# A first layer split as 128 + 64 rows, with paired half-array matmuls, separate id loads, a new order on the GpSimd queue and a later start of the expert slots

## The chip, the cores and the metric

The kernel runs on one core of a Trainium2 chip. The metric is device time in microseconds (us) of one execution. Each version was executed several times; executions of one kernel on one chip mostly agree within half a per cent. A run more than 1.5% above the fastest of its kernel is called slow and left out; the others are called fast. Every comparison is made within one set of runs on one chip, beside the kernel before on that same chip.

## The reference, cut to what matters

```python
# x: (8, 3584, 192); 28672 tokens of 192 numbers; 8 experts; F = 1024
w    = softmax(weight)                        # 8 heads x 7 taps
x    = causal_conv(x, w)                      # every head: 24 channels
e    = argmax(x @ w_gate)                     # one expert for each token
gate = softmax(x @ w_gate)[e]
eom  = sigmoid(x @ w_output_gate)             # only [e] is used
out  = gate * eom[e] * (relu(x @ w1[e]) @ w2[e])   # 192 -> 1024 -> 192
```

## The kernel before

The tokens are handled in 16 **units** of 1792. For each unit a **front** convolves, computes the logits, picks experts, and sorts the rows by expert. The sorted rows, scaled by the gate, with the token's id in two extra columns, are scattered by GpSimd into a stream in HBM, eight scatters a unit. From the stream they are loaded transposed, 512 rows of one expert at a time, and each such **slot** passes through the expert's two layers. A slot has four **quarters**. Four slots run in every unit, interleaved with the fronts of later units; the last unit takes all that is left, and a loop at the end takes whatever rows did not fill a slot.

The first layer has 192 input rows, and the array takes 128. So the kernel loads rows 0 to 127 into `xa`, the other 64 rows and padding into `xb`, and spends two full matmuls on each of eight chunks of 128 outputs:

```python
def load_w(e):                                    # before
    o = e * WE
    nc.gpsimd.dma_start(wres[:, o:o + F], moe_w1[e, 0:128, :])
    nc.gpsimd.dma_start(wres[0:64, o + F:o + 2 * F], moe_w1[e, 128:D, :])
    ...                                           # w2; rows 64..127 are zeroed by zero_w

def slot_load(base, u):
    ...
    i = nc.sync.dma_start_transpose(xa, xcg[bass.ds(base, TT), 0:128])
    i = nc.sync.dma_start_transpose(xb, xcg[bass.ds(base, TT), 128:256])

class Slot:
    def first(self, q):                           # a quarter of the first layer
        pp = ps_h.tile([128, 2, 512], FP32, tag="ph", name="pp")
        for j in range(2):
            fc = 2 * q + j
            nc.tensor.matmul(pp[:, j, :], self.w(fc * 128, 128), self.xa,
                             start=True, stop=False)
            nc.tensor.matmul(pp[:, j, :], self.w(F + fc * 128, 128), self.xb,
                             start=False, stop=True)
        ...                                       # ReLU into ht, on ScalarE or VectorE

    def second(self, q):
        ...                                       # eight matmuls of 192 columns
        if q == 1:                                # token ids, from a column of xb
            for j in range(4):
                nc.tensor.matmul(self.pp[:, 2 * D + j:2 * D + j + 1],
                                 self.xb[:, j * 128:(j + 1) * 128], idw,
                                 start=False, stop=(j == 3))
        if q % 2 == 1:
            nc.scalar.copy(out=self.y[:, q - 1:q + 1, :], in_=...)
            for j in (q - 1, q):
                emit_in()                         # at most one waiting scatter
                i = nc.gpsimd.indirect_dma_start(out=out, ...)   # 128 output rows
```

Scatters are not issued where their rows are made. They wait in a list, `pend`, and `emit_in()` issues one. The traces show GpSimd issuing its transfers in program order, so this Python order is the order of the queue. The main schedule starts the slots at unit 1:

```python
prev = None
for u in range(1, NU):
    todo = []
    for e, bap, inv in plans.pop(u):
        base = reg(bap, [ET.SP], E * CAP - TT)
        todo.append((e, inv, slot_load(base, u)))
    fa = front_a(u + 2) if u + 2 < NU else iter(())
    fb = front_b(u + 1) if u + 1 < NU else iter(())
    for k, (e, inv, xab) in enumerate(todo):
        ...
        s = Slot(xab, w_at(e * WE), inv)
        for q in range(4):
            s.first(q)
            drain(fa, 1)                          # one piece of a front
            if prev is not None:
                prev.second(q)
            drain(fb, 1)                          # one piece of another front
        prev = s
    drain(fa); drain(fb)
    emit_in(len(pend))
...
with tc.For_i(0, rn, 1):                          # slots chosen at run time
    ...
```

## Time and profile before

| kernel before | value | where it is read |
|---|---|---|
| time, median of 3 | 780.03 us | runs |
| profiled execution | 773.92 us, span 772.0 us | run, profile |
| TensorE busy | 85% of the span | busy totals |
| first slot starts | 86.1 us | timeline |
| one unit, mean of units 2 to 13 | 43.1 us | timeline |
| wait for `xa` where units meet | 2.3 to 3.0 us, units 2 to 14; 6.4 us at unit 15 | timeline |
| one slot with nothing beside it | 6.19 us | timeline of the tail |
| clock granted to TensorE, mean of each of units 2 to 14 | 0.96 (nine units) or 1.00 (four) | windows |

The profile has five engines: PE is TensorE (PEld its weight loads), DVE VectorE, ACT ScalarE, POOL GpSimd, and SP only issues transfers. A line of a timeline gives start, duration, engine, source line, operation, what it writes and reads, and the shape. A bracket at its end tells how long the engine was idle before it and what ended that. Matmuls are pipelined, so the distance from one start to the next is the cost, and the listed duration is not. The prediction shows the lines that carry the argument.

### The profile page before, as it was taken

What the parts mean: (1) busy time and instruction counts of PE and PEld (TensorE: products, weight loads), DVE (VectorE), ACT (ScalarE), POOL (GpSimd) and SP (SyncE); (2) the same over time, 40 slices, a digit from 0 to 9 for tenths busy, and PEclk for the clock granted to TensorE, in tenths of its full rate; (3) what the DMA queues carried; (4) which work ended last, traced back from release to release, by engine and by line L of the source; (5) the groups of instructions that cost most, each with busy time, mean ns of one, the idle gap of its engine ahead of it and who ended that gap; (6) DMA issues with size and microseconds to landing.
All of it is one profiled execution on the core that took longest, in us unless ns stands there. A gap on an engine that the chain in (4) does not pass through costs nothing. (4 is left out here: it accounts for less than half of the span.)

```text
span 772.0 us, 14134 instructions
## 1 busy us (share of the span) xinstructions
PE 655.4 (85%) x4948; PEld 436.2 (57%) x4948; DVE 406.5 (53%) x1298; ACT 366.5 (47%) x581; POOL 411.5 (53%) x425
## 2 busy tenths in 40 slices
PE   3866498989989898989989898989989898869953
PEld 1524165665757475656747475656757575547632
DVE  7425183836566383837556383837566474802220
ACT  0657153554535363545536364545546354436621
POOL 1436145473747465473737465563737375656652
PEclk9978599999999999999999999999999999989987
DMA  7999933253535343252535343442532313234110
GB/s 152 231 238 203 142 101 108 72 160 75 144 102 143 103 133 104 69 155 73 152 92 139 99 127 106 101 133 62 157 88 74 93 61 110 70 102 114 48 41 9
DMA packets 132359, 86.59 MB, mean 112 GB/s; under 512 B 88427, under 2 KB 122455, under 8 KB 132288
## 3 DMA queue, kind: packets, MB, share of 16 engines
q1 hardware_dynamic: 102656, 42.35, 23.4%
q0 software_dynamic: 28736, 43.31, 20.5%
q8 instruction: 39, 0.64, 0.4%
q14 instruction: 32, 0.26, 0.1%
q10 hardware_dynamic: 896, 0.03, 0.1%
HBM read 35.80 MB, written 44.43 MB: 104 GB/s over the span
## 5 line engine op out<-in xcount | busy, mean ns | idle before, releaser
L579 POOL DMA_INDIRECT out_dram<-y,oi x260 | 262.7, 1011 | 242.1 <-issue 179.0
L547 ACT ACTIVATE ht<-pp 128x1024 f16<-128x1024 f32 x195 | 199.3, 1022 | 183.9 <-PE pp L541 183.9
L539 PE MATMUL pp<-xa,wres 128*128 128x512 f16 x520 | 203.0, 390 | 61.1 <-DMA xa<-xcg_sorted 61.1
L558 PE MATMUL pyt<-wres,ht 128*128 128x192 f16 (+1 forms) x2080 | 220.9, 250 | 2.9 <-DVE ht L545 2.9
L558 PEld LDWEIGHTS <-ht 128*128 128x128 f16 x2080 | 182.7, 99 | 67.1 <-issue 37.0
L541 PE MATMUL pp<-xb,wres 128*128 128x512 f16 x520 | 202.2, 389 | 12.2 <-DMA xb<-xcg_sorted 12.2
L457 POOL DMA_INDIRECT xcg_sorted<-xs,du x128 | 130.1, 1017 | 89.4 <-ACT xs L278 42.2
L290 PE MATMUL pf<-xt,band 118*112 118x384 f32 x256 | 115.3, 543 | 19.5 <-DMA xt<-in_x_dram 14.1
L539 PEld LDWEIGHTS <-wres 128*128 128x128 f16 (+1 forms) x520 | 51.4, 99 | 112.4 <-DMA xa<-xcg_sorted 41.2
L545 DVE TENSOR_SCALAR ht<-pp 128x1024 f16<-128x1024 f32 x65 | 79.2, 1219 | 59.2 <-PE pp L541 59.2
L569 ACT COPY y<-pyt 128x384 f32<-128x384 f32 x130 | 62.4, 480 | 93.9 <-PE pyt L558 84.1
L280 DVE COPY cv<-pf 112x384 f32<-112x384 f32 x54 | 29.2, 541 | 89.3 <-PE pf L290 89.3
L290 PEld LDWEIGHTS pf<-xt,band 118*112 118x112 f32 x256 | 48.0, 195 | 48.9 <-DVE band L133 13.6
L541 PEld LDWEIGHTS <-wres 128*128 128x128 f16 (+1 forms) x520 | 51.8, 100 | 37.6 <-issue 8.2
L572 DVE TENSOR_SCALAR oi<-pyt 128x4 uint32<-128x4 f32 x65 | 10.5, 162 | 115.8 <-ACT y L569 110.3
L439 PE MATMUL pf<-xrow,pm 112*128 112x194 f16 x512 | 64.6, 247 | 6.9 <-DVE pm L423 4.5
L418 DVE TENSOR_TENSOR xrow<-cv,gs 112x384 f16<-112x384 f32 x128 | 64.7, 545 | 0.0
L423 DVE TENSOR_SCALAR pm<-pos,pos 112x256 f16<-112x256 f16 x256 | 64.6, 324 | 0.0
L304 PEld LDWEIGHTS pf<-identf,cv 112*128 112x128 f32 x384 | 43.6, 141 | 17.4 <-DVE cv L280 2.2
L278 ACT COPY cv<-pf 112x384 f32<-112x384 f32 x74 | 33.9, 479 | 40.1 <-PE pf L290 25.0
L304 PE MATMUL pf<-identf,cv 112*128 112x112 f32 x384 | 51.5, 260 | 0.5 <-ACT cv L278 0.4
L278 ACT CAST xs<-pf 128x388 f16<-128x388 f32 x76 | 37.2, 489 | 28.8 <-PE pf L439 20.2
(132 smaller groups left out, 425.0 us busy)
## 6 DMA issues: line engine op xcount, KB each, us to landing
xt<-in_x_dram SPq DMA_DIRECT2D x8, 1344.0 KB
xt<-in_x_dram SPq DMA_DIRECT2D x8, 1260.0 KB
out_dram<-y,oi POOLq DMA_INDIRECT x260, 2.7
wres<-in_moe_w_dram POOLq DMA_DIRECT2D x8, 384.0 KB, 10.5
wres<-in_moe_w_dram POOLq DMA_DIRECT2D x8, 256.0 KB, 11.5
xcg_sorted<-zrow SPq DMA_DIRECT2D x8, 256.0 KB
xcg_sorted<-xs,du POOLq DMA_INDIRECT x128, 3.2
xa<-xcg_sorted SPq DMA_TRANSPOSE x65
```

Of the source, the lines that this page charges most:

```text
L278: nc.scalar.copy(out=o, in_=i)
L290: nc.tensor.matmul(pc[0:BT, 0:NB * GH], band[0:KI, h, :], xt[0:KI, :, h * GH:(h + 1) * GH], start=True, stop=True)
L304: nc.tensor.matmul(pt[:, j * BT:(j + 1) * BT], cvf[0:BT, m * 2 * D + i * 128:m * 2 * D + (i + 1) * 128], identf[0:BT, 0:BT], is_transpose= ...
L418: nc.vector.tensor_tensor(out=xr[P, k:k + 2, 0:D], in0=cv[P, k:k + 2, :], in1=gs[P, k:k + 2].unsqueeze(2).to_broadcast([BT, 2, D]), op=ALU ...
L423: nc.vector.tensor_scalar(out=pms[i][P, l, :], in0=pos16[P], scalar1=pos[P, l * NG + i:l * NG + i + 1], scalar2=None, op0=ALU.is_equal)
L457: i = nc.gpsimd.indirect_dma_start(out=xcg2, out_offset=bass.IndirectOffsetOnAxis(ap=du[:, i:i + 1], axis=0), in_=xs.rearrange("p r w -> p ...
L539: nc.tensor.matmul(pp[:, j, :], self.w(fc * 128, 128), self.xa, start=True, stop=False)
L541: nc.tensor.matmul(pp[:, j, :], self.w(F + fc * 128, 128), self.xb, start=False, stop=True)
L545: nc.vector.tensor_relu(out=ht, in_=pp)
L547: nc.scalar.activation(out=ht, in_=pp, func=AF.Relu)
L558: nc.tensor.matmul(self.pp[:, o:o + D], self.ht[fc // 2][:, fc % 2, q * 128:(q + 1) * 128], self.w(2 * F + fc * D, D), start=(fc == 0 and ...
L579: i = nc.gpsimd.indirect_dma_start(out=out, out_offset=bass.IndirectOffsetOnAxis(ap=self.oi[:, j:j + 1], axis=0), in_=self.y[:, j, :], in_ ...
```

## The change

The intent is to save a quarter of the first layer's streaming. `xb` now holds columns 64 to 191. An even chunk takes rows 0 to 127 in one full matmul and has rows 128 to 191 left; an odd chunk takes rows 64 to 191 and has rows 0 to 63 left. The two 64-row remainders lie on different halves of the array and are meant to run side by side. Four full matmuls become two full ones and a pair. As `xb` no longer holds the ids, a third transfer `xi` loads them.

```diff
@@ weights @@
+    WA = F + F // 2
+    def load_w(e):
+        ... wres[:, o:o + F] as (g, l, c): rows 0..127 (l=0) or 64..191 (l=1)
+        for p0, d0, l in ((0, 0, 1), (64, 128, 0)):      # the 64-row remainders
+            nc.gpsimd.dma_start(
+                wres[p0:p0 + 64, o + F:o + WA].rearrange("p (g c) -> p g c", c=128),
+                bass.AP(... offset=w.offset + d0 * F + l * 128, ...))
@@ slot_load @@
-        i = nc.sync.dma_start_transpose(xb, xcg[bass.ds(base, TT), 128:256])
+        i = nc.sync.dma_start_transpose(xb, xcg[bass.ds(base, TT), 64:192])
+        i = nc.sync.dma_start(
+            xi, xcg[bass.ds(base, TT), IDC:IDC + 2].rearrange("(j p) w -> p j w", p=128))
@@ Slot.first @@
-            for j in range(2): ... two full matmuls for each chunk
+            nc.tensor.matmul(pp[:, 0, :], w[:, o:o + 128], self.xa, start=True, stop=False)
+            nc.tensor.matmul(pp[:, 1, :], w[:, o + 128:o + 256], self.xb, start=True, stop=False)
+            nc.tensor.matmul(pp[:, 0, :], w[64:128, c:c + 128], self.xb[64:128],
+                             start=False, stop=True)
+            nc.tensor.matmul(pp[:, 1, :], w[0:64, c:c + 128], self.xa[0:64],
+                             start=False, stop=True)
@@ Slot.second @@
-                for j in range(4): ... id matmuls against idw
-                for j in (q - 1, q):
-                    emit_in()
-                    i = nc.gpsimd.indirect_dma_start(out=out, ...)
+                pout.extend((self.y, self.oi, j) for j in (q - 1, q))
@@ schedule @@
-    NXS = 6
+    NXS = 10                                             # scatter buffers
+    U0 = 2                                               # slots start at unit 2
+    ND = 3                                               # run-time slots laid out statically
-    for u in range(1, NU):
+    for u in range(U0, NU):
+        if u == NU - 1:
+            for sel, bap, inv in [pick() for _ in range(ND)]:
+                ... todo.append((w_dyn(sel), inv, slot_load(base, u)))
                 if prev is not None:
                     prev.second(q)
+                    emit_out()                           # outputs, right after their copy
                 drain(fb, 1)
+                emit_in(len(pend))                       # every scatter that is ready
@@ run-time slots @@
+    def w_dyn(sel):
+        wd = pwd.tile([128, WE], FP16, tag="wd", name="wd")   # 2 buffers
+        nc.sync.dma_start(wd, wres[:, bass.ds(reg(sel...), WE)])   # 768 KB
+        return wd
```

Five things thus change together: the matmuls of the first layer, the ids, the order on the GpSimd queue, the start and the end of the slots, and the prologue (two experts' weights ahead of the first front instead of four).

## The prediction

> **What bounds the kernel now.** The kernel convolves, routes and sorts 16 units of 1792 tokens (the "front"), then runs 512-row slots, each through one expert's two layers. I read the page's busy totals first, then its slices, the groups, the waits, and the timeline of single units.
>
> ```profile
> PE 655.4 (85%) x4948; PEld 436.2 (57%) x4948; DVE 406.5 (53%) x1298; ACT 366.5 (47%) x581; POOL 411.5 (53%) x425
> PE   3866498989989898989989898989989898869953
> DMA  7999933253535343252535343442532313234110
> L539 PE MATMUL pp<-xa,wres 128*128 128x512 f16 x520 | 203.0, 390 | 61.1 <-DMA xa<-xcg_sorted 61.1
> L541 PE MATMUL pp<-xb,wres 128*128 128x512 f16 x520 | 202.2, 389 | 12.2 <-DMA xb<-xcg_sorted 12.2
> L565 PE MATMUL pyt<-idw,xb 128*128 128x1 f16 x260 | 15.7, 164 | 0.0
> ```
>
> TensorE leads at 85%, and its only long waits are for xa and xb, the transposed loads: 61.1 + 12.2 us. The first 96 us (five slices of 19.3 us) are different: DMA is at 7 to 9 tenths and TensorE low. The 1040 first-layer matmuls are listed at 390 ns, but they are pipelined; the timeline gives the true pitch. Here are the end of one unit and the first matmul of the next; columns are start us, duration, engine, line, what.
>
> ```profile
> 295.27 0.38 PE L541 MATMUL pp<-xb,wres 128*128 128x512 f16 x1
> 295.58 1.71 PE L313 MATMUL pf<-tt,wg 128*32 128x448 f32 x16
> 297.22 0.83 PE L558 MATMUL pyt<-wres,ht 128*128 128x192 f16 x8
> 297.89 0.38 PE L539 MATMUL pp<-xa,wres 128*128 128x512 f16 x1
> 298.11 0.38 PE L541 MATMUL pp<-xb,wres 128*128 128x512 f16 x1
> ...
> 299.19 0.82 PE L558 MATMUL pyt<-wres,ht 128*128 128x192 f16 x8
> 302.82 0.39 PE L539 MATMUL pp<-xa,wres 128*128 128x512 f16 x1 [2.81 <-DMA xa<-xcg_sorted]
> ```
>
> First-layer matmuls start 0.216 us apart, and eight second-layer ones take 0.66 us. In the tail, where nothing else runs, a quarter slot (4 + 8 matmuls) lasts 1.52 us (713.40 to 714.92), the quarter with the id matmuls 1.63, so a slot is 3 x 1.52 + 1.63 = **6.19 us**. Units begin at 129.9, 173.7, ... 604.7, 647.6: 43.1 us each on average over twelve, of which 2.6 us is the xa wait at the boundary. What feeds that wait is the POOL queue:
>
> ```profile
> 296.68 0.98 POOL L457 DMA_INDIRECT xcg_sorted<-xs,du  x1 [0.30 <-issue]
> ```
>
> Here POOL starts the unit's last scatter; its lines follow each other every 1.285 us, scatters and output rows alternating, 24 a unit (31 us). Its data were ready near 291; it stood in line. The load issues at 299.19, 2.5 us after the scatter's start, and TensorE resumes at 302.82, 6.1 us after it.
>
> **What the Trainium skill says.** "TensorEngine Tiling (Array Packing)", Key Properties: changing the tiling mode drains TensorE; tiles run independently. The trace agrees. Before the column-tiled L313, the last matmul should end at 295.27 + 0.216 = 295.49, but L313 starts at 295.58: 0.09 us. L313 is eight fp32 matmuls of 448 columns in four column tiles. One fp32 matmul of 384 columns takes 0.65 us here (L290), so eight would take 6.1 us serially and two rounds 1.5; it takes 1.64. Tiles do overlap; entry and exit together cost about 0.2 us. The 64-row matmuls L385 and L386 say the same: 0.09 late on entry (96.06 against 95.94 + 0.03), 0.085 late on exit (96.28 against 96.13 + 0.066).
>
> "TensorE: Matmul & The Clock Gate", Measured speedup vs the span model: a row-tiled pack takes one matmul's duration plus about 4 ns per tile. No row-tiled pair runs before the change, so the trace cannot say. The same page, Part 1: about 3.4 us of idleness halves the clock. The trace agrees in part: after the 2.5 us gap at 259.1, first-layer pitch is soon 0.43, until 264, and the units so hit have mean clock 0.96 instead of 1.00.
>
> "DMA: Bandwidth & Descriptors", Specifications: line rate needs 512 B per transfer. The new id load has runs of 4 B; no transfer of that kind is in this trace.
>
> **The change, part by part.** The diff does five things.
>
> 1. First layer. Per quarter slot four full matmuls become two full and two half-row ones meant to run together. Removed: one stream, 0.216 us. Added: entry 0.09 + exit 0.085 + weight-load stagger, estimated at 0.01 to 0.05. Net gain about 0.03 us a quarter, **0.12 a slot**, not the 0.86 that counting streams promises.
>
> 2. Ids. L565 goes: 0.11 us a slot. Three small vector operations (0.16 us each) replace two; a third SP transfer per slot joins two issued 1.45 us apart. SP has room. Slot: 6.19 - 0.12 - 0.11 = **5.96 us**.
>
> 3. POOL order. Scatters are issued as soon as their rows are ready and outputs right after their copy. The scatter chain after group 0 becomes 15 x 1.285 = 19.3 us instead of 21.6, so the boundary wait mostly goes. Unit: 43.1 - 2.6 (wait) - 0.6 (clock, half the units losing 1.3 or so) - 4 x 0.23 = 39.0. The chain itself (five quarters to group 0, about 12.3, + 0.7 + 19.3 + 6.1 = 38.4) is nearly as long, so I add 0.7 for imperfect meeting: **39.7 us**.
>
> 4. Slots start at unit 2, not 1. Replaying the routing on the reference's inputs, I count 60 static slots, three chosen at run time but laid out statically, and zero loop iterations after; before there were 64 static and one loop iteration. Two slots (12 us) and the serial loop go. A chosen slot copies its 768 KB of weights first, with two buffers: the third copy can begin only when the first chosen slot has finished. TensorE then waits about 2 us start + 768 KB at some 200 GB/s (best prologue rate is 254) + transposes behind it: estimated 8 us, plus 1.7 for the clock.
>
> 5. Prologue. One more front before the first slot, but only two experts' weights ahead of it instead of four, and ten scatter buffers instead of six. Fronts took 19.5 us (28.5 to 48) and 25 with DMA-starved waits; then came 13.4 us until xa, with DMA still full. I take 28.5 + 3 x 19.5 + 10 = **97 us** against 86. By bytes: 17.2 MB moved by 86 us, 2.5 MB more at 230 GB/s also gives 97.
>
> Sum: first slot at 97; units 2 to 13, 12 x 39.7 = 476.4; unit 14, with no convolution beside it, 37.5 (39.6 before, POOL-bound: 24 x 1.285 = 31 plus the ramp); unit 15, 10 x 5.96 + 9.7 wait + 6.0 + last second layer 2.7 = 78; end, 12.7 (before: 4.6 from the last matmul to the last output's end, 6.1 to the span's end; 2 for the skipped loop). Span 702. Timed runs before lie 8.0 over the profiled span (780.03 against 772.0), so **710 us**.
>
> **Rivals.** *The pair overlaps and the drain hides*: slot 5.22 us, 0.74 less. For it: the span model, and that 0.09 was seen with other shapes. It would save 47 us at most, but POOL (5.14 us a slot in the tail, 31 a unit) and the scatter chain would hold some: 670. *The halves do not overlap*: each quarter pays 0.18 more, 63 x 0.7 = 44 us: 755, still faster through parts 3 and 4. *POOL or the scatter chain becomes the bound*: units stay at 42 to 43 us; for it, POOL's unbroken row from 278 to 303; against it, 31 us of work in 40. It gives 740 to 745. *The 4-byte id loads clog the shared DMA engines and delay xa*: for it, 512 tiny runs a slot; against it, DMA is only 3 to 5 tenths busy in the steady part; +10 us.
>
> **Range and chances.** Parts 3 and 4 rest on counted waits and slots, so faster is nearly sure. The pair's true cost is the main unknown (670 to 755 at the ends), then the prologue (90 to 108). Eight in ten: 668 to 740. Faster by over 2% 0.96, within 2% 0.03, slower 0.01.
>
> **What would show it right or wrong.** The pitch of a quarter slot in the tail: 1.49 if I am right, 1.30 if the pair is free, 1.66 if serial. The xa wait at unit boundaries: under 1 us. Unit starts 39.7 apart. First slot near 97. One TensorE gap of some 8 us before the last chosen slot, and no loop body. Wrong if the pair is free and POOL keeps pace (lower), or if boundary waits return (higher).

## The result, and the profile after

The changed kernel takes **729.65 us** (median of 4, 726.50 to 733.58) beside 779.99 us (median of 4, 778.27 to 781.78) for the kernel before in the same rounds. The ratio is 0.936 (95% interval 0.931 to 0.941). Here and below a ratio is the mean time of one kernel's fast runs over the mean time of the other's fast runs of the same rounds, so it is not quite the ratio of the medians.

These are lines of the page of the changed kernel: busy totals, the slices of TensorE, and groups of instructions.

```profile
PE 638.0 (87%) x4592; PEld 373.5 (51%) x4592; DVE 412.9 (56%) x1367; ACT 356.7 (49%) x575; POOL 409.6 (56%) x425
PE   3888259899899999999999999899997988699974
L599 PE MATMUL pp<-xa,wres 128*128 128x512 f16 x240 | 94.5, 394 | 45.1 <-DMA xa<-xcg_sorted 44.7
L604 PE MATMUL pp<-xa,wres 64*128 64x512 f16 x240 | 95.6, 398 | 0.0
L602 PE MATMUL pp<-xb,wres 64*128 64x512 f16 x240 | 95.6, 398 | 0.0
```

TensorE's busy time fell only by 17 us, from 655 to 638, though a quarter of the first layer's streams is gone. The wait for `xa` is still there: 45 us ahead of L599. In the slices the hole ahead of the first slot is deeper than before (2 in the fifth slice, 73 to 91 us), and the long middle is fuller.

This is one quarter slot in the tail of the changed kernel, from the timeline, and the start of the next quarter:

```profile
655.01 0.38 PE L599 MATMUL pp<-xa,wres 128*128 128x512 f16 x1
655.23 0.38 PE L600 MATMUL pp<-xb,wres 128*128 128x512 f16 x1
655.54 0.39 PE L602 MATMUL pp<-xb,wres 64*128 64x512 f16 x1
655.54 0.39 PE L604 MATMUL pp<-xa,wres 64*128 64x512 f16 x1
655.86 0.83 PE L629 MATMUL pyt<-wres,ht 128*128 128x192 f16 x8
656.53 0.38 PE L599 MATMUL pp<-xa,wres 128*128 128x512 f16 x1
```

The two halves do start together. But they start 0.31 us after the second full matmul, where a full matmul would have followed after 0.216. The second layer begins 0.32 us after them, again 0.10 late. The quarter lasts 1.52 us, as long as a plain quarter did before. A slot takes 6.08 us in place of 6.19, and those 0.11 us are the id matmuls.

Where the profiled span shrank, 772.0 to 731.9 us, is seen by stage:

| stage (us) | before | after | difference |
|---|---|---|---|
| start of unit 2's slots | 129.9 | 97.6 | -32.4 |
| units 2 to 13 | 12 x 43.1 | 12 x 41.8 | -15.9 |
| unit 14 | 39.6 | 41.1 | +1.4 |
| from unit 15 to the end | 84.7 | 91.5 | +6.7 |

Before, unit 1 had slots too; now those rows are taken later, which is why the tail grows. The first and last rows together are -25.6 us and belong to the schedule. The second is the steady part, where the scatter queue and the waits lie. (The differences sum to -40.1. The profiled execution before was 6 us below its median and the one after 4 us above, which is the rest of the 50.)

### The profile page after: what moved, and what is told of

It reads as the page before. It is cut to its first block, busy times and chain, and to the rows that moved or that the text cites. A ratio compares the mean times of both kernels' runs of the same rounds, so it can differ in the third digit from the quotient of the medians.

```text
span 731.9 us, 13609 instructions
## 1 busy us (share of the span) xinstructions
PE 638.0 (87%) x4592; PEld 373.5 (51%) x4592; DVE 412.9 (56%) x1367; ACT 356.7 (49%) x575; POOL 409.6 (56%) x425
## 5 line engine op out<-in xcount | busy, mean ns | idle before, releaser
L483 POOL DMA_INDIRECT out_dram<-y,oi x252 | 250.0, 992 | 214.8 <-ACT y L635 150.0
L629 PE MATMUL pyt<-wres,ht 128*128 128x192 f16 x1920 | 204.4, 250 | 1.1 <-DVE ht L608 1.1
L629 PEld LDWEIGHTS <-ht 128*128 128x128 f16 x2016 | 172.8, 99 | 62.2 <-issue 47.0
L599 PE MATMUL pp<-xa,wres 128*128 128x512 f16 x240 | 94.5, 394 | 45.1 <-DMA xa<-xcg_sorted 44.7
L296 PE MATMUL pf<-xt,band 118*112 118x384 f32 x256 | 117.2, 555 | 13.1 <-DMA xt<-in_x_dram 10.8
L600 PE MATMUL pp<-xb,wres 128*128 128x512 f16 x240 | 93.8, 391 | 8.1 <-DMA xb<-xcg_sorted 8.1
L604 PE MATMUL pp<-xa,wres 64*128 64x512 f16 x240 | 95.6, 398 | 0.0
L602 PE MATMUL pp<-xb,wres 64*128 64x512 f16 x240 | 95.6, 398 | 0.0
L602 PEld LDWEIGHTS <-wres 64*128 64x128 f16 x240 | 22.3, 93 | 117.3 <-issue 115.1
L296 PEld LDWEIGHTS pf<-xt,band 118*112 118x112 f32 x256 | 38.9, 186 | 46.1 <-issue 17.8
L445 PEld LDWEIGHTS <-pm 112*128 112x128 f16 x512 | 43.6, 97 | 14.3 <-DVE pm L429 12.1
L599 PEld LDWEIGHTS <-wres 128*128 128x128 f16 x240 | 23.8, 99 | 50.0 <-DMA xa<-xcg_sorted 27.3
```

The source lines that it names most:

```text
L296: nc.tensor.matmul(pc[0:BT, 0:NB * GH], band[0:KI, h, :], xt[0:KI, :, h * GH:(h + 1) * GH], start=True, stop=True)
L445: nc.tensor.matmul(ps[:, r * XW:(r + 1) * XW], pm[P, l, r * 128:(r + 1) * 128], xr[P, l * NG + i, :], start=(r == 0 and l == 0), stop=(r = ...
L483: i = nc.gpsimd.indirect_dma_start(out=out, out_offset=bass.IndirectOffsetOnAxis(ap=oi[:, j:j + 1], axis=0), in_=y[:, j, :], in_offset=Non ...
L599: nc.tensor.matmul(pp[:, 0, :], w[:, o:o + 128], self.xa, start=True, stop=False)
L600: nc.tensor.matmul(pp[:, 1, :], w[:, o + 128:o + 256], self.xb, start=True, stop=False)
L602: nc.tensor.matmul(pp[:, 0, :], w[64:128, c:c + 128], self.xb[64:128], start=False, stop=True)
```

## The experiments

The theory after the first reading had three parts. (1) The pair brings nothing as it is placed, because entering and leaving the half-array form costs what packing saves. (2) In the steady part, the next unit waits for the last scatter of this one, so the order on the GpSimd queue sets the pitch. (3) The later start and the missing loop give the rest. Rivals: the packing is the gain; the order is worth nothing; the id loads and the copied weights cost.

### First set, on a chip that turned out to be different

Here the kernel before took 802.32 us (median of 7, 801.15 to 806.37).

**The unedited changed kernel** as base of the set.

> The changed kernel itself, unedited, as the base of this set: 729 us and 0.936 of before, as measured. It gives the time of the changed kernel on the same chip and in the same rounds as the three kernels that undo one part of it.

It took 777.30 us, ratio 0.969 (0.964 to 0.973). The change gains 25 us here and 50 on the first chip. The trace of this set shows stalls that none of the other chips' traces have: VectorE stands idle for 5.90 us up to 401.56, ScalarE for 3.86 us up to 401.68, both with the releaser "remote", which the profile prints when it can name no instruction of this core behind the event. Beyond 100 us there are 9 such waits on VectorE (52.8 us) and 10 on ScalarE (29.3 us). Units are stretched to 44.8 us each on average and the waits for `xa` between them nearly vanish. What causes the stalls is open.

**Packing undone.** The remainders are zero-padded to full rows and run one after the other. Run-time slots read the weights in place, through a register, as before the change.

```diff
-    WA = F + F // 2
+    WA = F + F
+    wv = wres.rearrange("p (e w) -> p e w", w=WE)
+    nc.vector.memset(wv[0:64, :, F:F + F // 2], 0.0)
+    nc.vector.memset(wv[64:128, :, F + F // 2:2 * F], 0.0)
@@ Slot.first @@
-            nc.tensor.matmul(pp[:, 0, :], w[64:128, c:c + 128], self.xb[64:128], ...)
-            nc.tensor.matmul(pp[:, 1, :], w[0:64, c:c + 128], self.xa[0:64], ...)
+            nc.tensor.matmul(pp[:, 0, :], w(0, 128, c, 128), self.xb, ...)
+            nc.tensor.matmul(pp[:, 1, :], w(0, 128, c + F // 2, 128), self.xa, ...)
```

> The packing alone undone: the 64-row remainders are padded with zeros and run as two full-row matmuls, one after the other; ids, order and schedule stay as changed. (With no 64-row operand the run-time weights need no copy, so the wait before the last slot, 5.4 us and about 2 us of cold clock, goes too.) Theory, the drain eats the overlap: a quarter slot in the tail stays at 1.52 us within 0.02, unit pitch unchanged, total 722 us. Rival, the packing is what made the kernel faster: a quarter becomes 1.7 us, and 252 quarters cost 45 to 50 us more, total 765 to 775.

It took 779.28 us, ratio 0.972 (0.968 to 0.976): the same as the base within the intervals. That speaks against packing as the gain, but on a chip whose stalls set the pitch a difference at TensorE could hide. It was repeated below.

**The old order on the GpSimd queue.** One scatter before each output, as before the change.

```diff
-                pout.extend((self.y, self.oi, j) for j in (q - 1, q))
+                for j in (q - 1, q):
+                    emit_in()
+                    pout.append((self.y, self.oi, j))
+                    emit_out()
@@ schedule @@
-                emit_in(len(pend))
```

> The order on the GpSimd queue alone undone: scatters are issued one ahead of each output row block again, as before the change. Theory, the unit pitch is set by where the last scatter stands in that queue: the wait for xa at unit boundaries goes back from 1.3 to 2.5 us or more, unit pitch rises by 1 to 1.5 us over 13 units, total 742 to 750 us. Rival, the order does not matter because TensorE sets the pitch: within 4 us of the changed kernel.

It took 779.50 us, ratio 0.970 (0.963 to 0.977), one of its four runs slow and left out. There is no difference. As the units hardly wait for `xa` on this chip, the run could not tell the theories apart; it was repeated below as well.

**Slots from unit 1 again.** The start, the loop at the end and the number of slots as before, and so the order of experts in a unit; four experts' weights load during unit 1.

```diff
-    ND = 3
+    ND = 0
-    U0 = 2
+    U0 = 1
-            if u == U0 and k < 2:
-                load_w(E - 2 + k)
+            if u == U0:
+                load_w(EH + k)
```

> The schedule alone undone: slots start at unit 1 again, no slot is laid out for run-time choice, one pass of the loop remains. Theory, the schedule is a large part of the gain: first slot about 10 us earlier, one more unit (+41 us), three slots and the copy waits less in the last unit (-25 us), loop +20 us: total 750 to 758 us. Rival, the schedule is neutral and packing plus order made the gain: within 5 us of the changed kernel.

It took 799.80 us, ratio 0.996 (0.993 to 1.000). On this chip the schedule is thus worth 22 us, nearly all of the gain. Its trace tells how: unit 2 begins at 128.26 us instead of 97.84, 30.4 us later, and unit 15 needs 88.3 us to the end instead of 99.8, so 11.5 us come back and 19 remain. In the stage table of the first chip the start and the end are worth 25.6. The undoing is not pure: its one loop slot waits 11.1 us for the copy of its weights, where the loop slot of the kernel before waited 7.0 us for `xa`, so some 4 us of the 22 may belong to the copy.

### Second set

The kernel before took 781.41 us (median of 7).

**The unedited changed kernel** again.

> The changed kernel again, as the base of this set, because the first set ran on a chip where every kernel was slower (before 802 us) and its traces held stalls of 3 to 4 us in which VectorE and ScalarE stopped together. If this chip is like the first profile's: 726 to 734 us; if it is like the first set's: near 777.

It took 727.40 us, ratio 0.932 (0.928 to 0.937), as on the first chip, and without "remote" stalls.

**Outputs held while a unit's scatters are due.** Eight scatters of a unit become ready between the fifth and the twelfth quarter. Through those quarters only every second quarter lets one output go; the others follow the last scatter.

```diff
-    def emit_out():
+    def emit_out(n=99):
-        while pout:
+        while pout and n:
+            n -= 1
@@ schedule, in each quarter q of slot k @@
+                m = 4 * k + q
+                hold = u < NU - 1 and 4 <= m < 11
+                if not hold and m != 11:
                     emit_out()
                 drain(fb, 1)
                 emit_in(len(pend))
+                if m == 11:
+                    emit_out()
+                elif hold and m % 2 == 0 and m > 4:
+                    emit_out(1)
```

> One edit to the changed kernel: while a unit's eight scatters are due, output row blocks are held back (one every second quarter slot) and sent after the last scatter. Nothing is removed from the GpSimd queue; 24 entries a unit stay. Theory, the unit pitch is set by the last scatter's place in that queue: the last scatter starts about 4 us earlier, the xa wait at unit boundaries (1.1 to 3.8 us) vanishes, unit 14 loses most of its 6.8 us wait; 25 to 35 us less than the base of this set. Rival, TensorE already sets the pitch or the id loads delay xa: within 5 us of the base.

It took **687.53 us**, ratio 0.880 (0.876 to 0.884): 40 us less than the base of the set, more than the theory had asked for. A unit takes 38.7 us instead of 41.3. This is the whole table of TensorE's waits of this kernel for 250 to 555 us (eight units): it is empty. For the whole run, the list begins with this line; its columns are what waited, for what, total, times and longest:

```profile
PE pp L600 <- DMA xa<-xcg_sorted: 25.5, 3, 17.5
```

Of 15 waits for `xa` in the changed kernel (50.1 us) three are left: before the first slot, at unit 15, and 5.28 us ahead of the last run-time slot. The second part of the theory holds.

**The halves of two quarters together.** Two quarters' full matmuls run first, then both their pairs, so the form is switched twice a slot instead of four times.

```diff
-            for q in range(4):
-                s.first(q)
+                if q % 2 == 0:
+                    s.first2(q // 2)     # 4 full matmuls, then 2 pairs
```

> One edit to the changed kernel: the full-row matmuls of two quarter slots run first and their two pairs of halves after them, so the array enters and leaves the 64-row mode twice a slot instead of four times; the matmuls are the same. Theory, entry and exit cost 0.095 + 0.10 us each time: two quarters in the tail take 2.84 us instead of 3.04, 0.4 us a slot; the last unit's 11 slots gain 4 us and the front part of each unit about 0.5 us, while the rest of a unit stays tied to the scatters: 8 to 14 us less than the base. Rival, the 0.1 us gaps are the loading of weights and not a change of mode, so that halving the switches changes nothing: two quarters stay at 3.04 us and the time within 3 us of the base.

It took 725.23 us, ratio 0.929 (0.923 to 0.935): no difference from the base. The array did what the theory says. Two quarters in the tail, from its timeline:

```profile
652.27 0.38 PE L601 MATMUL pp<-xa,wres 128*128 128x512 f16 x1
652.49 0.38 PE L602 MATMUL pp<-xb,wres 128*128 128x512 f16 x1
652.80 0.39 PE L609 MATMUL pp<-xb,wres 64*128 64x512 f16 x1
652.80 0.39 PE L611 MATMUL pp<-xa,wres 64*128 64x512 f16 x1
653.02 0.38 PE L609 MATMUL pp<-xb,wres 64*128 64x512 f16 x1
653.03 0.38 PE L611 MATMUL pp<-xa,wres 64*128 64x512 f16 x1
653.34 1.49 PE L636 MATMUL pyt<-wres,ht 128*128 128x192 f16 x16
```

The second pair follows the first after 0.22 us, and the late start (0.31) and the late end (0.31) are paid once. These two quarters began at 651.84 and the next began at 654.67: 2.83 us instead of 2 x 1.52. The following two took 3.00, because a buffer was awaited for 0.18 us. TensorE's busy time fell by 16 us, from 629.7 us in the base of this set to 613.3. In the tail this counted: from unit 15 to the end it took 85.9 us instead of 90.7 in the base. In the units it did not: the waits for `xa` were there as in the base (1.1 to 3.1 us where units meet, 8.3 before unit 15), units 2 to 14 took 4.0 us more in all, and the first slot came 2.5 us later, so nothing was left of it in the total. The expectation had the tail right (4 us) and erred in the units, by taking time off TensorE for time off the kernel while another queue set the pitch.

**Everything together.** Outputs held, halves of two quarters together, only the 128 KB of remainders copied for a run-time slot (the rest read in place), and experts 4 and 5 asked for after unit 2's scatters instead of before.

```diff
-        wd = pwd.tile([128, WE], FP16, tag="wd", name="wd")
+        wd = pwd.tile([128, F // 2], FP16, tag="wd", name="wd")      # 3 buffers
-        if u < U0:
-            load_w(2 + 2 * u)
-            load_w(3 + 2 * u)
+        if u != 1:
+            load_w(2 + u)
+            load_w(3 + u)
```

> Both edits together, with two more: for run-time slots only the 64-row remainders (128 KB instead of 768) are copied, and the full-row weights are addressed through a register at partition 0, with three small buffers; and in the prologue the weights of experts 4 and 5 are asked for after the scatters of unit 2 instead of before them. Theory: units fall to TensorE's own 37 to 38.5 us, the wait before the last slot (5.4 us + 2 us of cold clock) goes, the first slot comes about 6 us sooner: 50 to 65 us less than the base. Rival, the scatter queue still binds at 24 x 1.285 us plus its start: less than 30 us gained.

It took **673.24 us** (671.79 to 675.23), ratio 0.863 (0.858 to 0.867), the fastest. The first slot starts at 89.5 us instead of 97.6, which only the order of the weights can have done, as nothing else edited runs before it. The gap ahead of the last run-time slot is gone. Slots in the tail take 5.83 us. But the pitch of the units stayed at 38.9 us, though their four slots are 1 us cheaper: from 250 to 555 us TensorE was busy 291.9 us of 305 and now waits for small steps of the front, above all evictions. The remaining long wait is 6.59 us at unit 15, for the vector operations that choose the run-time slots.

### Third set: the two questions of the first set, asked again

The kernel before took 775.33 us (median of 7).

> The changed kernel unedited, as the base of this set. A ratio to the kernel before of 0.93 to 0.94 (727 to 734 us beside 780) says that the chip is like the first one; 0.97 says that it is like the chip of the first set, on which the comparison of queue orders told nothing.

The **unedited changed kernel** took 728.40 us, ratio 0.938 (0.935 to 0.941), without "remote" stalls. The chip is like the first.

**Packing undone** (the same edit as above).

> Packing undone, everything else of the change kept: the 64-row remainders are zero-padded to full rows and run one after the other. Theory (the pair in place saves about 0.01 us of each quarter slot, as the drain on entry and exit takes what packing gives): within 1.5% of the unedited changed kernel, 718 to 735 us, quarter slots of 1.52 us in the tail. Rival (packing is what the change gains by: 240 quarters by 0.216 us saved is 52 us): 770 to 785 us, quarter slots of 1.7 us or more.

It took 723.41 us, ratio 0.934 (0.930 to 0.937). The intervals overlap; if anything it is faster than with packing. Its timeline of a quarter in the tail, four full matmuls and the second layer:

```profile
690.53 0.38 PE L603 MATMUL pp<-xa,wres 128*128 128x512 f16 x1
...
691.18 0.38 PE L608 MATMUL pp<-xa,wres 128*128 128x512 f16 x1
691.40 0.82 PE L633 MATMUL pyt<-wres,ht 128*128 128x192 f16 x8
692.06 0.38 PE L603 MATMUL pp<-xa,wres 128*128 128x512 f16 x1
```

A quarter lasts 1.53 us, and a slot 6.09 us instead of 6.08. **The pair is worth 0.01 us a slot.** The 5 us are near what the copied weights cost: the 5.2 us gap ahead of the last run-time slot does not exist here.

**The old order on the GpSimd queue** (the same edit as above).

> The changed kernel with the kernel before's order on the GpSimd queue: one scatter entry before each output. Theory (mid-run the unit waits for its last scatter, so an order that puts more outputs ahead of the scatters moves every unit later by about the entries moved): 740 to 755 us, waits for the first tile of a unit of 2 to 4 us instead of 1 to 3. Rival (the order is worth nothing, the start and the missing loop pass carry the gain): within 4 us of the unedited changed kernel.

It took 762.44 us, ratio 0.982 (0.980 to 0.985): 34 us more than the base, where the theory expected 12 to 27. A unit takes 44.3 us instead of the 41.6 of this set's base, so the twelve units make 32 of them. Compare one unit's scatters on POOL. In the changed kernel (first profile) the unit's slots start at 348.48 us and the next unit's at 389.01:

```profile
364.05 0.98 POOL L463 DMA_INDIRECT xcg_sorted<-xs,du  x1 [2.27 <-DVE tk L503]
...
367.95 0.98 POOL L463 DMA_INDIRECT xcg_sorted<-xs,du  x1 [0.30 <-DVE xs L286]
369.24 0.98 POOL L463 DMA_INDIRECT xcg_sorted<-xs,du  x1 [0.31 <-DVE ht L608]
...
383.38 0.98 POOL L463 DMA_INDIRECT xcg_sorted<-xs,du  x1 [0.30 <-issue]
```

With the old order they start at 362.60, and the next unit's at 407.14:

```profile
381.25 0.98 POOL L463 DMA_INDIRECT xcg_sorted<-xs,du  x1 [2.27 <-DVE tk L503]
...
385.14 0.98 POOL L463 DMA_INDIRECT xcg_sorted<-xs,du  x1 [0.30 <-DVE xs L286]
387.13 0.98 POOL L483 DMA_INDIRECT out_dram<-y,oi  x1 [1.01 <-ACT y L635]
388.42 1.27 POOL L463 DMA_INDIRECT xcg_sorted<-xs,du  x1 [0.30 <-issue]
...
401.57 0.98 POOL L463 DMA_INDIRECT xcg_sorted<-xs,du  x1 [0.30 <-issue]
```

Read each as a chain of three pieces. From first to last scatter: 19.33 us after the change, 20.32 with the old order. Among the latter is the wait at 387.13: POOL stands idle for an output whose `y` is not copied yet, while the scatter behind it has had its rows since 384.84 (the end of that eviction on VectorE). From the last scatter to the next unit's first matmul: 5.63 and 5.57, the same. From the unit's start to its first scatter: **15.57 and 18.65**. (The base of this set has 19.34, 5.86 and 15.63 for the same unit.) That third piece, 3 us longer, is not spent in the queue: POOL stands idle for 2.27 us before both first scatters. It is the clock. These are the windows of that one unit in both kernels; the columns are the window, its length, the busy time of PE, PEld, DVE, ACT and POOL, then the granted clock, the DMA share and GB/s. First the changed kernel:

```profile
348.48:389.01 40.53, 38.94 (x290) 23.13 (x291) 24.53 (x78) 21.40 (x34) 23.91 (x25) 1.00 0.44 120
```

Then the old order:

```profile
362.60:407.14 44.54, 41.80 (x291) 24.16 (x291) 23.45 (x75) 21.51 (x34) 24.00 (x25) 0.92 0.41 107
```

The same 290 matmuls keep TensorE busy 2.9 us longer at a mean clock of 0.92. In that unit the clock is 0.51 to 0.56 up to 370.00 and 1.00 after. The waits ahead of units were 2.0 to 2.6 us with the old order (3.6 once) and every unit ran at 0.91 to 0.96; in the changed kernel nine of twelve are 1.0 to 1.7 us, and nine of the units 3 to 14 run at 0.96 to 1.00. A cold start lengthens its own unit and not the next wait: from the first scatter to the end of its work TensorE needs 23.64 us in both units shown, and the wait is what the chain and the load take beyond that, 1.32 and 2.25 us. So in this kernel the order costs a unit twice, once by the longer wait and once by the low clock after it. Over units 3 to 13, against the base of this set, the way to the first scatter is 2.0 us longer on average, the chain 1.0 longer and the last piece 0.2 shorter. The expectation had only the queue. The kernel before had waits of 2.3 to 3.0 us and yet units of 0.96 and 1.00, so wait and clock do not go strictly together, and why it stayed warmer than this one is open.

**Packing undone and outputs held.** In this kernel TensorE sets the pitch, so a gain of packing could not hide.

> Packing undone and outputs held while a unit's scatters are due, together: here TensorE, not the scatter queue, sets the mid-run pitch, so a gain of packing could not hide. Theory (packing in place worth 0.00 to 0.01 us a quarter): a ratio to the kernel before of 0.875 to 0.885, as the packed kernel with held outputs had (0.880), so 683 to 692 us beside 781. Rival (packing worth something that the scatter queue hid, say 0.05 us a quarter, 12 us in all): a ratio of 0.895 or more, 699 us or more.

It took 679.11 us (678.35 to 680.14), ratio 0.876 (0.874 to 0.878). The packed kernel with held outputs had 0.880 (0.876 to 0.884) in its own set. Packing as built gains nothing where it should have gained most. A unit takes 38.1 us, half a us less than the 38.7 of the packed kernel. The groups of both for 250 to 555 us tell where. The packed kernel, where the convolution's matmuls are L296:

```profile
L296 PE MATMUL pf<-xt,band 118*112 118x384 f32 x128 | 57.6, 532 | 0.0
```

And the kernel with full rows, where the same matmuls are L298:

```profile
L298 PE MATMUL pf<-xt,band 118*112 118x384 f32 x128 | 51.8, 486 | 0.0
```

128 convolution matmuls, which in part follow a pair, took 532 ns on average with pairs and 486 without, at a clock of 1.00 in both: 5.8 us over eight units. In the steady part leaving the pair can thus cost more than in the tail. The two runs come from different chips, but the base and the full-rows kernel of the third set, on one chip, give the same two means in their units 6 and 8, at a clock of 1.00.

## Why the prediction was right, and where it was wrong

The sum was right within 20 us: 710 predicted, 729.65 measured, in the range. By its own steps:

1. **First layer.** Right in its mechanism. Entry was put at 0.09 and measured at 0.095, exit at 0.085 and 0.10, the stagger at 0.01 to 0.05 and 0.00 to 0.01. The net gain of 0.03 us a quarter was mis-sized: it is at most 0.01, and the full-rows kernels show that it is worth nothing in time. The Trainium skill's "TensorEngine Tiling (Array Packing)", Key Properties, says that a change of mode drains; the two switches cost 0.195 us of the 0.216 that the pair saves. Two of the named rivals, free overlap and serial halves, are excluded by quarter slots of 1.52 us, the halves starting together.

2. **Ids.** Right: the slot lost 0.11 us (6.19 to 6.08). The rival of slow id loads was not tested by itself; the fact that held outputs alone remove the waits, with the id loads in place, leaves it little room.

3. **POOL order.** The right lever, mis-sized on both sides. The predicted unit of 39.7 us measured **41.8**: 25 us over twelve units, the main miss. It rested on "the boundary wait mostly goes" with a chain of 38.4 us and 0.7 for imperfect meeting. The reading of the clock was low too: eight of the twelve units before ran at 0.96, which is some 1.7 us each (estimate: 0.04 of 43), and not half of them at 1.3. The waits stayed at 1.0 to 3.8 us, 1.7 on average. In the unit shown the chain of scatters was 19.33, exactly as predicted, and the last piece 5.63 (6.1 predicted); the first piece was 15.57 where the prediction had 12.3 + 0.7. So the step that failed is the time up to the first scatter. Part of it is VectorE: the first group's rows were done on TensorE by 361.57 us, but VectorE, busy without a gap since 358, came to them only at 363.22, and the scatter followed at 364.05:

```profile
360.95 0.62 PE L445 MATMUL pf<-xrow,pm 112*128 112x194 f16 x4
363.22 0.56 DVE L286 CAST xs<-pf 128x388 f16<-128x388 f32 x1
```

   Units alternate: in units 5 and 7, also at a clock of 1.00, the first piece was 13.7 and 13.8, but the chain 20.4. The seven units in the middle (5 to 11) average 40.7 us, 1.0 over the prediction; the first three and the last two average 43.4, 3.7 over. The sum, 7 x 1.0 + 5 x 3.7, is the 25 us. Of those five, four ran at a clock of 0.92 to 0.96, which the prediction had written off with the wait; the fifth (at 0.99) had POOL idle for 2.19 us between a scatter and an output, and ended in a wait for `xa` of 3.75 us. The rival "POOL or the scatter chain becomes the bound", 740 to 745, was the true mechanism: holding the outputs takes 40 us off. The old order shows the other side: without this part the change would have gained 13 us instead of 47.

4. **Start at unit 2.** Right: 60 static and three run-time slots, no loop body in the trace. The wait for the third copy was put at 8 us and is 5.39, in this line of the changed kernel's timeline:

```profile
710.73 0.58 PE L599 MATMUL pp<-xa,wd 128*128 128x512 f16 x1 [5.39 <-DMA xa<-xcg_sorted]
```

   The same matmul takes 0.58 us instead of 0.38: the clock is low up to 716 us, as foreseen. "TensorE: Matmul & The Clock Gate", Part 1, gives about 3.4 us of idleness; 5.39 us agree, while waits of 2.0 to 2.6 us had already cooled the units of the old-order kernel. Units 14 and 15 came out longer than predicted, 41.1 for 37.5 (it ends in a wait for `xa` of 6.82 us) and 81.5 for 78; the end, put at 12.7, took 10.0.

5. **Prologue.** 97.57 measured, 97 predicted, but by luck in its first working. The three fronts ended at 79.75 us, not at 87, and the wait for `xa` after them took 17.8 us, not 10:

```profile
78.54 1.21 PE L445 MATMUL pf<-xrow,pm 112*128 112x194 f16 x8 [0.98 <-DVE pm L429]
97.57 0.58 PE L599 MATMUL pp<-xa,wres 128*128 128x512 f16 x1 [17.82 <-DMA xa<-xcg_sorted]
```

   The second working took the prologue as bound by bytes; the fastest kernel, in which that wait is 10.4 us, shows that about 8 us of it were only the order in which two experts' weights stood.

6. **The offset.** The 8.0 us added for "timed runs lie over the profiled span" was an error: it compared the median with one profiled execution that was itself 6 us fast. Time is span plus 1.7 to 1.9 us within one execution. This error added, and hid 6 of the 30 us by which the span had been put too low. Without it the sum is 704, still inside the range.

In the end the gain is not where the change's name has it. In the runs that tell the parts apart, the order on the GpSimd queue carries 34 us, start and end 22 to 26, and the pair with its copied weights nothing or a few us the other way. The values come from different sets, and the parts interact, so they need not add up to the 47 to 54 us measured for the whole on those chips that did not stall. The id loads and the ten scatter buffers were not undone by themselves.

## What to carry to other kernels

Before packing small matmuls, count the switches of form: one pair between full matmuls saved 0.216 us of streaming and paid 0.195, while two pairs in a row save twice that and pay once. Before saving on the busiest engine, find the chain that closes the loop: here rows, scatter queue, load and next unit; saved TensorE time stayed invisible in the units, while moving outputs behind the scatters brought 40 us at once. A short wait in a loop should be priced with the low clock that can follow it: in the old-order kernel that cost 2.0 us a unit, and the longer chain 1.0.

## What the Trainium skill lacked or had wrong

- "TensorEngine Tiling (Array Packing)", Key Properties: it names the drain at a change of mode and gives no size. Here, between 128-row matmuls and a pair of 64-row ones: 0.095 us on entry and 0.10 us on exit, against 0.216 us saved by a pair.
- "TensorE: Matmul & The Clock Gate", Measured speedup vs the span model: the few ns per tile agree (the halves start 0.00 to 0.01 us apart), but the speedup is that of packs alone. Among full matmuls a single pair gave 6.08 us a slot against 6.09 without packing, and two pairs in a row 5.83.
- The same page, Part 1: idle time of about 3.4 us is given for the lower clock. In the unit of the old-order kernel that was looked at closely, a wait of 2.30 us was followed by a clock of 0.51 to 0.56 for 7 us, and every unit of that kernel, after waits of 2.0 to 3.6 us, ran at a mean of 0.91 to 0.96; after waits of 1.0 to 1.5 us in the changed kernel most units ran at 1.00. The length of the wait alone does not decide: in the kernel before, after waits of 2.3 to 3.0 us, four of thirteen units ran at 1.00.
- No page gives the pitch at which GpSimd issues indirect transfers of 128 rows: 1.285 us each here, for scatters and outputs alike, in program order. An output whose data were not ready held back a scatter that was ready, for 1.01 us in the case shown.
- No page tells how far chips differ: the same kernel took 775 to 802 us on four chips, and on the slowest VectorE and ScalarE stopped together with the releaser "remote" (9 and 10 waits, 52.8 and 29.3 us). Its cause is open.
